# One transposing load for four token tiles, in a routed mixture of experts

## The chip, the cores and the metric

The kernel runs on one core of one Trainium2 chip. The metric is the device time of one execution in microseconds (us), as the median of several runs. [...]

## What is computed

The input `x` has 8 sequences of 3584 tokens with 192 channels, all float32. First a causal convolution of seven taps runs along each sequence; its taps are a softmax over one weight row per head, and each of the 8 heads owns 24 channels. The 28672 rows of the result then go through a mixture of 8 experts with one expert for each token:

```python
xn = x / (norm(x) + 1e-6); en = expert_emb / (norm(expert_emb) + 1e-6)
logits = xn @ en.T / tau
e = argmax(logits);  gate = softmax(logits)[e]
out = gate * (relu(x @ w1[e]) @ w2[e])       # w1: 192 x 1024, w2: 1024 x 192
```

## The kernel before, in words

Tokens are worked on in 16 chunks of 1792 (`CT`): 16 tiles (`NT`) of 112 tokens (`TP`), one token a partition. Chunk by chunk there are two parts.

The first part prepares and routes. `load_x` brings the chunk's rows (one DMA of about 1.5 MB, with a small one ahead where a sequence begins). `mix` runs the convolution as matmuls with a band matrix (L389), copies the result back over the input (L392) and sums squares (L402, L405). `scaled` multiplies four tiles (a group, `GX`) by a power of two and casts them to float16 into `rows2` (L436, L438); `rest` adds the float16 remainders that keep near-float32 precision and repeats 64 columns (L445, L448, L451). `rows2` holds two chunks; a token's row has 240 words of 32 bits there (`RW`): 448 float16 columns, then the token's number and its gate (words 224 and 225), then zeros. `turn` transposes a group: the first 384 float16 columns of each of its four tiles become three blocks of 128 channels by 112 tokens in `xtb`, a ring of four groups. `logits` multiplies these blocks by the expert embeddings (L612), `rank` finds each token's expert, its gate and its row in a list sorted by expert, and `put` sends the rows of one tile to that list in DRAM, `rows_d`, with an indirect DMA from GpSimd (L628). The first two chunks are transposed on TensorE instead (L499, L503), and their groups lie in the same ring.

The second part runs the experts over blocks of 128 to 512 rows of one expert. `fetch` reads the block's place (L745) and loads its rows from `rows_d`, transposed, with two DMAs on SyncE's queue (L753), and a small load of numbers and gates (L757). The loads name the scatters that they need. Three blocks are held. `expert` then runs the first product with five matmuls for each of eight column chunks (L799), the ReLU on ScalarE (L803) and its float16 remainder on VectorE (L805), then the second product for each 128 rows (L822), the gate on ScalarE (L827, into `y`, a ring of four tiles of 128 by 192 float32), and an indirect DMA from GpSimd to the output (L829). The first product's five PSUM banks (`h`) serve the second product too.

Which blocks are run is chosen while the chunks still come in: after chunks 2, 3, 5, 8 and 12 (`PICK`), and at the end, `hand_out` or `last_blocks` calls `pick` and that `select`, a chain of some twenty tiny VectorE instructions on one partition (L663 to L712). It writes `sel`, which SyncE (L745), TensorE and VectorE read for each block.

The order of the work is planned in Python: `run` walks through an expert's steps, counts a clock of its own, and draws steps of the routing in between. After the last `turn` of a chunk the plan waits 14 of its microseconds (`TURN`) before the logits. SyncE's instructions stay in the order in which they are written: turn of groups 0 and 1, `load_x` of the chunk two ahead, turn of groups 2 and 3, and the fetches between them. The other engines' instructions are put in order by the tile framework with a simulated timeline, and each engine runs its list in order.

GpSimd's DMAs build their descriptors in a scratch area of SBUF, 8192 bytes a partition.

Of the kernel before, what the change touches and what calls it, by code (L numbers as in the profile page):

```python
# [12 lines left out]
F16 = mybir.dt.float16  # L13
# [12 lines left out]
D = 192  # L26
# [5 lines left out]
CT = TP * NT  # L32
XD = 224
RW = 240


W2 = 3 * F
# [5 lines left out]
NFC = F // 128  # L43
PICK = (2, 3, 5, 8, 12)
GX = 4
XW = GX * 3 * TP
NACT = 3
PRE = 39
TURN, RANK, GAP = 14.0, 10.0, 0.5
# [26 lines left out]
class _Moe:  # L76
    def __init__(self, ctx, tc, x, weight, emb, tau, w1, w2, out):
        self.tc, self.nc = tc, tc.nc
        self.x, self.weight, self.emb, self.tau = x, weight, emb, tau
        self.w1, self.w2, self.out = w1, w2, out  # L80
        B, S, _ = x.shape
        self.B, self.S, self.N = B, S, B * S
        self.nch = self.N // CT
        self.per_b = S // CT
        self.cap = self.N + PAD
        self.dummy = E * self.cap
        pool = lambda name, bufs, **k: ctx.enter_context(
            tc.tile_pool(name=name, bufs=bufs, **k))
        self.cp = pool("const", 1)
        self.xp = pool("xload", 2)  # L90
        self.sp = pool("small", 2)
        self.lp = pool("lone", 1)
        self.ep = pool("expert", 3)
        self.yp = pool("y", 3)
        self.op = pool("out", 4)
        self.mp = pool("meta", 6)
        self.rings = {k: pool("ps_" + k, n, space=PSUM)
                      for k, n in (("r", 2), ("l", 1), ("h", 5))}

        self.res = self.cp.tile([128, E * RES], F16, name="res")  # L100
        self.work = self.cp.tile([128, 2 * NFC * 512 + S2 + RES - W2], F16, name="work")
        self.hid = self.work[:, 0:2 * NFC * 512]
        self.slot = self.work[:, 2 * NFC * 512:]
        self.xtb = self.cp.tile([128, NT // GX, XW + HALO], F16, name="xtb")
        self.rows2 = self.cp.tile([TP, 2, NT, RW], I32, name="rows2")
        self.ids = self.cp.tile([TP, NT], I32, name="ids")
        self.xtn = 0
        self.wexp = self.cp.tile([128, E, 2], I32, name="wexp")
        self.dp = pool("scratch", 1, space=DRAM)
        self.rows_d = self.dp.tile([E * self.cap + PAD, RW], I32, name="rows_d")  # L110
        self.scatters, self.pend, self.step = [], [], None
        self.nput, self.final = 0, False
        self.counts, self.pace = {}, 1.0
        self.xts, self.mixed = [], {}
        self.subs, self.ready, self.at, self.copied = [], 0, 0, 0
        self.clock, self.mm = 0.0, None
# [50 lines left out]

    def constants(self):
        nc, cp = self.nc, self.cp
        nc.gpsimd.memset(self.xtb[:, :, XW:], 0.0)  # L170
        nc.gpsimd.memset(self.rows2[:, :, :, XD + 2:], 0)
        nc.gpsimd.iota(self.ids, pattern=[[TP, NT]], base=TP - 1,
                       channel_multiplier=-1)
        head = self.ep.tile([128, 4 * 512], F16, tag="xT", name="head")[:].bitcast(F32)
        self.idf, self.onef = head[:, 0:128], head[:, 128:256]
        make_identity(nc, self.idf)
        self.idh = cp.tile([128, 128], F16, name="idh")
        nc.vector.tensor_copy(out=self.idh, in_=self.idf)
        nc.gpsimd.memset(self.onef, 1.0)
        self.oneh = cp.tile([128, 128], F16, name="oneh")  # L180
        nc.gpsimd.memset(self.oneh, 1.0)

        self.lth = cp.tile([128, 128], F16, name="lth")
        nc.gpsimd.memset(self.lth, 1.0)
        nc.gpsimd.affine_select(
            out=self.lth, in_=self.lth, pattern=[[1, 128]], base=0,
            channel_multiplier=-1, compare_op=ALU.is_gt, fill=0.0)

        tmp = self.op.tile([128, D], F32, tag="y", name="tmp")[:, 0:2 * E + 64].bitcast(I32)
        e8i = tmp[0:TP, 0:E]  # L190
        nc.gpsimd.iota(e8i, pattern=[[-1, E]], base=E, channel_multiplier=0)
        self.e8 = cp.tile([TP, E], F32, name="e8")
        nc.vector.tensor_copy(out=self.e8, in_=e8i)

        self.rst = cp.tile([TP, E, NT], F32, name="rst")
        nc.gpsimd.memset(self.rst, 1.0)
        nc.gpsimd.memset(self.rst[:, :, 0:1], 0.0)

        nums = tmp[0:1, E:E + 64]
        nc.gpsimd.iota(nums, pattern=[[1, 64]], base=0, channel_multiplier=0)  # L200
        self.nums = cp.tile([1, 64], F32, name="nums")
        nc.vector.tensor_copy(out=self.nums, in_=nums)

        cbi = tmp[:, E + 64:]
        nc.gpsimd.iota(cbi, pattern=[[self.cap, E]], base=0, channel_multiplier=0)
        self.cb = cp.tile([128, E], F32, name="cb")
        nc.vector.tensor_copy(out=self.cb, in_=cbi)

        self.start = cp.tile([1, E], F32, name="start")
        nc.vector.tensor_copy(out=self.start, in_=cbi[0:1, :])  # L210
# [231 lines left out]
    def rest(self, c, g):  # L442
        xc, u = self.mixed[c][0], slice(g * GX, g * GX + GX)
        rows = self.rows2[:, c % 2].bitcast(F16)
        self.nc.vector.tensor_tensor(  # L445
            out=rows[:, u, 0:128], in0=xc[:, u, 0:128],
            in1=rows[:, u, 128:256], op=ALU.subtract)
        self.nc.vector.tensor_tensor(  # L448
            out=rows[:, u, 320:384], in0=xc[:, u, 128:192],
            in1=rows[:, u, 256:320], op=ALU.subtract)  # L450
        self.nc.vector.tensor_copy(out=rows[:, u, 384:448], in_=rows[:, u, 256:320])  # L451


    def route(self, c):
# [23 lines left out]
    def first(self, c):  # L478
# [9 lines left out]
        for v in steps:  # L488
# [4 lines left out]
            else:  # L493
# [4 lines left out]
                for a in range(GX):  # L498
# [2 lines left out]
                        in_=rows[:, g * GX + a, k * 128:(k + 1) * 128],  # L501
                        identity=self.idh[:TP, :TP])
                nc.scalar.copy(  # L503
                    out=xT[:, 0:XW].rearrange("p (a k t) -> p a k t", k=3, t=TP)[:, :, k, :],
                    in_=tp)
                if k == 2:
                    if g == 0:
# [6 lines left out]
    def rank(self, c, lg, f):  # L514
# [63 lines left out]
        di = sp.tile([TP, NT], I32, tag="di", name="di")  # L578
        nc.vector.tensor_single_scalar(out=di, in_=dr, scalar=-1.0, op=ALU.add)
        yield 0.8, 0.0  # L580
        self.pend += [(c, di[:, t:t + 1], r32[:, t, :]) for t in range(NT)]
        self.left += CT
        if c + 1 in PICK[1:]:
            self.hand_out(c + 1)
# [23 lines left out]
    def logits(self, lg, xT, g):  # L608
        for a in range(GX):
            for k in range(3):  # L610
                u = (a * 3 + k) * TP
                i = self.nc.tensor.matmul(  # L612
                    out=lg[:, g * GX + a, :], lhsT=xT[:, u:u + 128],
                    rhs=self.mb if k == 2 else self.ma,
# [4 lines left out]

    def turn(self, c, g):  # L620
        xT, rows, t = self.xt_next(), self.rows2[:, c % 2].bitcast(F16), g * GX
        xv = xT[:, 0:XW].rearrange("p (a k t) -> p a k t", k=3, t=TP)
        for a in range(GX):
            self.nc.sync.dma_start_transpose(out=xv[:, a], in_=rows[:, t + a, 0:2 * D])
        return xT

    def scatter(self, idx, src):
# [29 lines left out]
    def select(self, n, k, last, name, cb):  # L657
# [17 lines left out]
        nc.vector.scalar_tensor_tensor(out=bs, in0=ap, scalar=-float(n),  # L675
                                       in1=self.start, op0=ALU.mult, op1=ALU.add)
        jf = self.nums[:, 0:k]
        ge, df = one("ge", (1, k, E + 1), F16), one("df", (1, k, E))
        nc.vector.memset(ge, 1.0)
        nc.vector.tensor_tensor(  # L680
            out=ge[:, :, 1:], in0=a[:].unsqueeze(1).to_broadcast([1, k, E]),
# [3 lines left out]
        nc.vector.tensor_tensor(  # L685
            out=df, in0=df, in1=bs[:].unsqueeze(1).to_broadcast([1, k, E]),
            op=ALU.mult)
        ro, tm, se = one("ro", (1, k)), one("tm", (1, k)), one("se", (1, k))
        nc.vector.tensor_reduce(out=ro, in_=df, op=ALU.add, axis=AX.X)
        nc.vector.scalar_tensor_tensor(out=ro, in0=jf, scalar=float(n), in1=ro,  # L690
                                       op0=ALU.mult, op1=ALU.add)
# [353 lines left out]
```

## Time and profile before

| | us |
|---|---|
| median of 3 runs (lowest, highest) | 1233.92 (1232.15, 1236.98) |
| the profiled execution | 1238.18 |
| its span, first to last instruction | 1236.5 |
| TensorE matmul busy | 1127.5 (91%) |
| VectorE busy | 756.1 (61%) |
| ScalarE busy | 587.4 (48%) |
| GpSimd busy | 550.4 (45%) |
| mean granted TensorE clock | 0.955 |

Busy time of TensorE is from the start of a matmul to its modelled end, so it is no measure of peak speed, but the time in which it has nothing under way is idle time. The transposing loads of `turn` lie between 124.7 and 766.7 us of the span. Before that the weights are prepared and the first two chunks are routed; after it, only experts' blocks are left.

### The profile page before, as it was taken

Reading aid. Unit: us, or ns where it says so; the run is one execution under the profiler, and the core shown is the slowest. Engines: PE = TensorE matmul, PEld = TensorE weight load, DVE = VectorE, ACT = ScalarE, POOL = GpSimd, SP = SyncE. Lnnn points to the kernel's source line nnn. Section 1 sums busy time; section 2 is a strip of 40 time slices with the busy share of each in tenths; the row PEclk is TensorE's granted clock in tenths of the full one; section 3 lists DMA queues with packets and bytes.
Section 4 is the critical chain, followed back from the end, with each engine's and each line's share of the span. In section 5 each row is a group of like instructions: output and inputs, shape, how many; then the busy total and the mean of one; then the engine's idle time right before and its main releaser. Section 6 shows DMA issues by size and latency. Waiting matters only on the chain.

```text
span 1236.5 us, 31375 instructions
## 1 busy us (share of the span) xinstructions
PE 1127.5 (91%) x10428; PEld 872.4 (71%) x10428; DVE 756.1 (61%) x2029; ACT 587.4 (48%) x1350; POOL 550.4 (45%) x522
## 2 busy tenths in 40 slices
PE   4675769899999899998989999999999999999998
PEld 2553658786677876756877676666677777898897
DVE  2899766886668757666675746553434453466365
ACT  4986445554554555563635454423333333333333
POOL 0074165574575645565745546673222222222222
PEclk9676879899999999999989999999999999999999
DMA  9945566576675576755638545326122231123121
GB/s 243 231 131 157 119 157 150 126 164 122 150 173 146 109 158 134 161 144 107 164 73 191 110 86 134 90 87 107 43 54 49 52 72 49 44 48 71 43 57 43
DMA packets 305818, 140.68 MB, mean 114 GB/s; under 512 B 247630, under 2 KB 296141, under 8 KB 305664
## 3 DMA queue, kind: packets, MB, share of 16 engines
q1 hardware_dynamic: 282000, 87.97, 34.3%
q0 software_dynamic: 23664, 50.68, 14.5%
q8 instruction: 94, 1.54, 0.5%
q14 instruction: 60, 0.49, 0.1%
HBM read 38.35 MB, written 51.05 MB: 72 GB/s over the span
## 4 chain that ended last, share of the span: by engine, by line
PE 37%; issue 8%; POOL 3%; DMA 3%; ACT 1%; DVE 1%; POOLq 0%; ACTq 0%; DVEq 0%
PE h_ps L799 18%; PE o_ps L822 17%; POOL out_dram L829 2%; POOL rows_d L628 1%; PE conv_ps L389 1%; DMA rows_d<-rows,di 1%; DMA xtb<-rows 1%; DMA out_dram<-y,e_mt 1%; ACT work L803 1%; DVE work L805 0%; DMA rows_d<-xtb,padi 0%; ACT rows L438 0%; ACT sq L402 0%; PE lg_ps L612 0%; DVE work L735 0%
## 5 line engine op out<-in xcount | busy, mean ns | idle before, releaser
L822 PE MATMUL o_ps<-work 128*128 128x192 f16 x5472 | 497.8, 248 | 21.3 <-DVE work L805 9.9
L822 PEld LDWEIGHTS <-work 128*128 128x128 f16 x5472 | 458.5, 99 | 59.9 <-DVE work L805 15.9
L829 POOL DMA_INDIRECT out_dram<-y,e_mt x228 | 255.1, 1119 | 470.8 <-ACT y L827 434.0
L805 DVE SCALAR_TENSOR_TENSOR work<-h_ps,work 128x512 f16<-128x512 f32 x456 | 311.1, 687 | 169.0 <-ACT work L803 165.2
L803 ACT ACTIVATE work<-h_ps 128x512 f16<-128x512 f32 x456 | 267.5, 596 | 236.5 <-PE h_ps L799 205.5
L628 POOL DMA_INDIRECT rows_d<-rows,di x256 | 281.6, 1100 | 141.4 <-issue 56.8
L799 PE MATMUL h_ps<-e_xT,res 128*128 128x512 f16 x1360 | 312.3, 382 | 6.9 <-DVE work L805 3.5
L799 PEld LDWEIGHTS <-res 128*128 x1360 | 131.8, 98 | 162.0 <-issue 19.7
L799 PE MATMUL h_ps<-e_xT,work 128*128 128x256 f16 (+1 forms) x2200 | 226.7, 259 | 15.2 <-DMA e_xT<-rows_d 10.2
L799 PEld LDWEIGHTS <-work 128*128 128x128 f16 x2200 | 187.4, 99 | 41.5 <-DMA e_xT<-rows_d 10.4
L827 ACT ACTIVATE y<-o_ps,g 128x192 f32<-128x192 f32 x228 | 92.8, 418 | 236.2 <-PE o_ps L822 209.7
L735 DVE COPY work<-res 128x3074 f16 x85 | 82.3, 968 | 165.2 <-PE o_ps L822 161.2
L389 PE MATMUL conv_ps<-xt,band 128*112 128x384 f32 x256 | 110.8, 534 | 14.9 <-ACT xt L392 8.0
L438 ACT CAST rows<-xt 112x768 f16<-112x768 f32 x64 | 53.0, 832 | 97.3 <-DMA rows_d<-rows,di 44.5
L392 ACT COPY xt<-conv_ps 112x384 f32<-112x384 f32 x128 | 60.3, 479 | 43.7 <-PE conv_ps L389 41.2
L402 ACT ACTIVATE sq<-xt 112x192 bf16<-112x192 f32 x204 | 73.6, 361 | 4.8
L445 DVE TENSOR_TENSOR rows<-xt,rows 112x512 f16<-112x512 f32 x64 | 44.2, 690 | 45.0 <-ACT rows L438 42.5
L389 PEld LDWEIGHTS conv_ps<-xt,band 128*112 128x112 f32 x256 | 42.7, 193 | 33.3 <-issue 14.5
L436 DVE TENSOR_TENSOR xt<-xt,x_p_s 112x768 f32<-112x768 f32 x64 | 58.6, 953 | 0.0
L732 DVE COPY work<-res 128x3072 f16 x56 | 53.7, 960 | 0.2 <-PE h_ps L799 0.2
L612 PEld LDWEIGHTS <-xtb 128*128 128x128 f16 x768 | 30.2, 98 | 26.7 <-DMA xtb<-rows 13.2
L612 PE MATMUL lg_ps<-ma,xtb 128*128 128x16 f16 x512 | 31.0, 171 | 14.3 <-ACT xtb L503 7.5
(158 smaller groups left out, 524.7 us busy)
## 6 DMA issues: line engine op xcount, KB each, us to landing
xt<-in_dram SPq DMA_DIRECT2D x8, 1536.0 KB
xt<-in_dram SPq DMA_DIRECT2D x7, 1440.0 KB
rows_d<-rows,di POOLq DMA_INDIRECT x256
out_dram<-y,e_mt POOLq DMA_INDIRECT x228
xtb<-rows SPq DMA_TRANSPOSE x224
res<-in_dram SPq DMA_DIRECT2D x4, 768.0 KB
work<-in_dram SPq DMA_DIRECT2D x4, 768.0 KB
e_xT<-rows_d SPq DMA_TRANSPOSE x184
```

Source lines behind the costliest of these rows:

```text
L389: self.behind(nc.tensor.matmul(out=ps, lhsT=self.band[:, h, :], rhs=xt[:, :, h * G:(h + 1) * G], start=True, stop=True))
L392: nc.scalar.copy(out=xc[:, :, h * G:(h + 1) * G], in_=ps)
L402: nc.scalar.activation(out=sq, in_=xc[:, t, :], func=AF.Square, accum_out=n2[:, t:t + 1])
L612: i = self.nc.tensor.matmul(out=lg[:, g * GX + a, :], lhsT=xT[:, u:u + 128], rhs=self.mb if k == 2 else self.ma, start=(k == 0), stop=(k = ...
L628: i = self.nc.gpsimd.indirect_dma_start(out=self.rows_d[:, :], out_offset=bass.IndirectOffsetOnAxis(ap=idx, axis=0), in_=src, in_offset=No ...
L735: self.nc.vector.tensor_copy(out=self.slot[:, S2:], in_=self.res[:, bass.ds(self.we + W2, RES - W2)])
L799: mm = nc.tensor.matmul(out=ps[:, c, :], lhsT=w1(o, b + c), rhs=xT[:, k, :], start=(i == 0), stop=(i == 4))
L803: self.step = nc.scalar.activation(out=hh[:, b:b + m, :], in_=ps, func=AF.Relu).ins
L805: nc.vector.scalar_tensor_tensor(out=hl[:, b:b + m, :], in0=ps, scalar=0.0, in1=hh[:, b:b + m, :], op0=ALU.max, op1=ALU.subtract)
L822: mm = nc.tensor.matmul(out=o, lhsT=h[:, c, q], rhs=w2[:, c, k:k + D], start=(c + i == 0), stop=(c == NFC - 1 and i == 2))
L827: self.step = nc.scalar.activation(out=y, in_=o, func=AF.Copy, scale=g[:, a:a + 1]).ins
L829: i = nc.gpsimd.indirect_dma_start(out=self.out[:, :], out_offset=bass.IndirectOffsetOnAxis(ap=mt[:, a, 0:1], axis=0), in_=y, in_offset=No ...
```

## The change

The rows in `rows2` get 256 words, so that a group's four tiles are, in each partition, one run of 2048 float16 columns: 16 blocks of 128. `turn` loads a group with one transposing DMA in place of four. A tile has four blocks in `xtb` now, of which the fourth (the repeated columns, the word pair and zeros) is not used by the logits; the 16 columns behind a tile's third block, which the third block's matmul reads along, lie at the start of the fourth. The scatters still send 240 words of a row. L451 copies 68 columns a tile in place of 64, so that the word pair is written before the transpose reads it.

Room for this is made in two places: the scratch for GpSimd's descriptors is 4096 bytes a partition, and the larger temporary tiles of `select` (`ge`, `df`, and `ro`, `tm`, `se` inside the first) are taken from the ring of `y`.

```diff
+SW = 256
-XW = GX * 3 * TP
+XW = GX * 4 * TP
...
-        self.xtb = self.cp.tile([128, NT // GX, XW + HALO], F16, name="xtb")
-        self.rows2 = self.cp.tile([TP, 2, NT, RW], I32, name="rows2")
+        self.xtb = self.cp.tile([128, NT // GX, XW], F16, name="xtb")
+        self.rows2 = self.cp.tile([TP, 2, NT, SW], I32, name="rows2")
...
-        nc.gpsimd.memset(self.xtb[:, :, XW:], 0.0)
+        nc.gpsimd.memset(self.xtb[:].rearrange(
+            "p h (a k t) -> p (h a) k t", k=4, t=TP)[:, :, 3, 0:HALO], 0.0)
...
-        self.nc.vector.tensor_copy(out=rows[:, u, 384:448], in_=rows[:, u, 256:320])
+        self.nc.vector.tensor_copy(out=rows[:, u, 384:452], in_=rows[:, u, 256:324])
...
-        self.pend += [(c, di[:, t:t + 1], r32[:, t, :]) for t in range(NT)]
+        self.pend += [(c, di[:, t:t + 1], r32[:, t, 0:RW]) for t in range(NT)]
...
-                u = (a * 3 + k) * TP
+                u = (a * 4 + k) * TP
...
     def turn(self, c, g):
         xT, rows, t = self.xt_next(), self.rows2[:, c % 2].bitcast(F16), g * GX
-        xv = xT[:, 0:XW].rearrange("p (a k t) -> p a k t", k=3, t=TP)
-        for a in range(GX):
-            self.nc.sync.dma_start_transpose(out=xv[:, a], in_=rows[:, t + a, 0:2 * D])
+        self.nc.sync.dma_start_transpose(
+            out=xT.rearrange("p (n t) -> p n t", t=TP),
+            in_=rows[:, t:t + GX, :].rearrange("p a c -> p (a c)"))
         return xT
...
-        ge, df = one("ge", (1, k, E + 1), F16), one("df", (1, k, E))
+        tmp = self.op.tile([128, D], F32, tag="y", name="sl_ge")[0:1]
+        ro, tm, se = (tmp[:, i * k:(i + 1) * k] for i in (5, 6, 7))
+        ge = tmp.bitcast(F16)[:, 0:k * (E + 1)].rearrange("p (k e) -> p k e", e=E + 1)
+        df = self.op.tile([128, D], F32, tag="y", name="sl_df")[0:1, 0:k * E].rearrange(
+            "p (k e) -> p k e", e=E)
...
-        ro, tm, se = one("ro", (1, k)), one("tm", (1, k)), one("se", (1, k))
...
-                    dynamic_dma_scratch_size=8192)
+                    dynamic_dma_scratch_size=4096)
```

## Rows read from the trace of the kernel before

**Rows 1.** The page's part 2: tenths in 40 slices of 30.9 us.
```profile
PE   4675769899999899998989999999999999999998
PEclk9676879899999999999989999999999999999999
DMA  9945566576675576755638545326122231123121
```

**Rows 2.** Waits of PE: us in total, times, longest.
```profile
PE lg_ps L612 <- DMA xtb<-rows: 11.7, 9, 3.7
...
PE h_ps L799 <- DMA e_xT<-rows_d: 10.2, 2, 6.0
```

**Rows 3.** Source lines L624 and L753: SyncE's time for one, ns min/median/max.
```profile
L624 SPq DMA_TRANSPOSE xtb<-rows x224: 1174/1252/4145, 124.7 to 766.7; - x112
...
L753 SPq DMA_TRANSPOSE e_xT<-rows_d x184: 1130/1236/2622, 113.0 to 1229.9; - x184
```

**Rows 4.** Timeline, chunk 2's first turn: start, us, instruction, idle before.
```profile
124.73 10.27 SPq L624 DMA_TRANSPOSE xtb<-rows  x8
...
127.09 0.21 PE L612 MATMUL lg_ps<-ma,xtb 128*128 128x16 f16 x2 [3.67 <-DMA xtb<-rows]
```

**Rows 5.** Windows, one quiet fetch: busy of the engines, PEclk, DMA share, GB/s.
```profile
1053.50:1054.00 0.50, 0.50 (x9) 0.50 (x7) 0.00 (x0) 0.00 (x0) 0.00 (x0) 1.00 0.79 172
```

**Rows 6.** Timeline, chunk 3's second turn and the fetch behind it.
```profile
164.77 0.52 SPq L373 DMA_DIRECT2D xt<-in_dram  x1
165.39 12.24 SPq L624 DMA_TRANSPOSE xtb<-rows  x8
...
173.67 0.22 PE L612 MATMUL lg_ps<-ma,xtb 128*128 128x16 f16 x2 [3.08 <-DMA xtb<-rows]
...
178.41 2.53 SPq L753 DMA_TRANSPOSE e_xT<-rows_d  x2
...
181.51 4.87 PE L799 MATMUL h_ps<-e_xT,work 128*128 128x256 f16 x22 [6.02 <-DMA e_xT<-rows_d]
```

**Rows 7.** Windows there: last three columns PEclk, DMA share, GB/s.
```profile
168.00:170.00 2.00, 2.00 (x33) 2.00 (x30) 1.94 (x19) 0.81 (x5) 1.39 (x3) 1.00 1.07 349
170.00:172.00 2.00, 0.59 (x14) 0.36 (x10) 2.00 (x4) 0.42 (x1) 2.00 (x1) 1.00 1.22 348
...
180.00:185.00 5.00, 3.49 (x17) 2.50 (x18) 2.56 (x11) 0.83 (x1) 3.78 (x5) 0.50 0.95 146
```

**Rows 8.** Timeline, chunk 4's second turn and the fetch behind it.
```profile
209.24 14.72 SPq L624 DMA_TRANSPOSE xtb<-rows  x8
...
224.83 2.53 SPq L753 DMA_TRANSPOSE e_xT<-rows_d  x2
...
228.94 2.32 PE L799 MATMUL h_ps<-e_xT,work 128*128 128x256 f16 x10 [4.16 <-DMA e_xT<-rows_d]
```

**Rows 9.** Window right behind it, columns as in Rows 5.
```profile
230.00:235.00 5.00, 5.00 (x38) 3.76 (x37) 3.10 (x8) 1.19 (x2) 3.20 (x4) 0.56 0.70 161
```

**Rows 10.** Timeline, chunk 6's second turn.
```profile
308.28 12.89 SPq L624 DMA_TRANSPOSE xtb<-rows  x8
...
321.89 0.18 PE L612 MATMUL lg_ps<-mb,xtb 128*128 128x16 f16 x1 [1.53 <-DMA xtb<-rows]
```

**Rows 11.** Waits of SyncE's queue: us in total, times, longest.
```profile
SPq L364 <- DVE rows L448: 25.1, 3, 10.4
```

**Rows 12.** Groups by line and form: VectorE's copy in `rest`.
```profile
L451 DVE COPY rows<-rows 112x256 f16<-112x256 f16 x64 | 14.1, 221 | 0.0
```

**Rows 13.** Timeline, `select` after chunk 2 and at the end, and `y`.
```profile
186.97 0.16 DVE L704 CAST sel<-sl_se 1x7 int32<-1x7 f32 x1 [2.11 <-SPq L745]
...
814.84 0.15 DVE L705 CAST sel<-sl_ro 1x8 int32<-1x8 f32 x1
...
827.42 0.42 ACT L827 ACTIVATE y<-o_ps,g 128x192 f32<-128x192 f32 x1 [5.38 <-DMA out_dram<-y,e_mt]
```

**Rows 14.** Timeline, GpSimd in a run of scatters.
```profile
181.75 0.94 POOL L628 DMA_INDIRECT rows_d<-rows,di  x1 [0.30 <-ACT rows L438]
```

More of the change, by code (lines that the diff above doesn't have):

```diff
@@ L503, in first @@
                 nc.scalar.copy(
-                    out=xT[:, 0:XW].rearrange("p (a k t) -> p a k t", k=3, t=TP)[:, :, k, :],
+                    out=xT[:, 0:XW].rearrange("p (a k t) -> p a k t", k=4, t=TP)[:, :, k, :],
                     in_=tp)
```

## The prediction

> **What bounds the kernel now.** I read the page's row of slices first: TensorE is 0.8 busy or more from the seventh slice on, nearly always at full clock, while it has holes in the first six, where the clock falls as well [rows 1]. So TensorE sets the end, and a change on SyncE's queue can only be worth what TensorE waits for that queue. The second view is TensorE's waits: it stood 11.7 us for the transposing loads of `turn` and 10.2 us for the experts' loads [rows 2]. This is the ceiling, 22 us, with some more where the clock falls behind a hole. The third view, the source lines, says why the loads come late: SyncE is held 1.25 us by each, and as long by a load of an expert's block: over blocks of 128 to 512 rows the median is 1.24 and the least 1.13 [rows 3]. Sixteen loads a chunk hold it 20 us or more, and whatever stands behind them waits. Then I went through the timeline of the four places that hold nearly all of this waiting.
>
> **The change, part by part.** A group's four loads become one. For 14 chunks that is 56 loads in place of 224. The issue time did not move with the size in the trace, so I take 1.25 us for one, which frees SyncE of 168 x 1.25 = 210 us; by itself this is worth nothing, since SyncE isn't the bound. The load moves 112 x 2048 x 2 = 459 KB where the four moved 344 KB. The nearest row for the speed is a fetch of a 512-row block with nothing beside it, 172 GB/s in its busiest half microsecond [rows 5]: 2.7 us, estimated. From issue to the first matmul the old load took 127.09 - 124.73 = 2.36 us [rows 4], of which 1.25 is issue, 0.5 its own 86 KB at that speed, and 0.6 the rest. The new one: 1.25 + 2.7 + 0.6 = 4.5 us.
>
> Place A, chunk 2's first turn [rows 4]. TensorE waits from 123.4. The first tile came at 127.09, the fourth after 3 x 1.28 more, at 130.9; the matmuls of the second product lay between them. Now all four come at 124.73 + 4.5 = 129.3: the first wait is 2.2 us longer, and the short ones for the second and third tile, at most the spacing of the issues (10.27/8 = 1.28) each, are gone. I take 0, with -2 and +3 as ends.
>
> Place B, chunk 3's second turn [rows 6]. Eight loads stand behind `load_x`'s 1.5 MB, and the fetch of the next block behind all of them. TensorE idles 3.08 us for the logits and then 6.02 us for the block. The DMA engines moved 348 GB/s there [rows 7]; 1.5 + 2 x 0.46 = 2.4 MB take 6.9 us, so the two loads land near 172.5 and SyncE is free at about 173, against 177.6. The fetch issues there in place of 178.41 and TensorE begins 3.1 us later as before, at 176.1 against 181.51. I take -5; the ends are 0 (something else holds the fetch) and -9 (both waits gone). The granted clock is 0.50 while TensorE works on after the hole [rows 7]; a hole of 5 us will leave it there, so nothing is taken for the clock.
>
> Place C, chunk 4's second turn [rows 8]. The loads hold SyncE from 209.24 to 223.96 and the fetch follows at 224.83; TensorE waits 4.16 us. By the sum for B the loads are through by 218, and the block is there by 221, before TensorE wants it at 228.94 - 4.16 = 224.8: -4.2. The hole is gone, and with it the clock of 0.56 in the five busy microseconds behind it [rows 9], 5 x 0.44 = 2.2 us. Together -6.4, ends 0 and -6.4.
>
> Place D, chunk 6 [rows 10]: eight loads of 12.89 us end after the planned 14 us, and a logit waits 1.53 us. Two loads behind `load_x` take some 8 us: -1.5, ends 0 and -3.5 (with the clock).
>
> What is late next: SyncE comes sooner to `load_x`, which waits until VectorE has read the older chunk (25.1 us in three waits now [rows 11]); that wait grows, but it ends when it ended, so the fetches behind are not later than before.
>
> The 33% more bytes: the DMA engines are 0.5 to 0.7 busy in those slices [rows 1]; scatters and fetches share them. I take 0, with +3 as the upper end (a seventh of the 22 us of waits, as rough as that).
>
> L451 copies 272 columns for 256: 221 ns x 16/256 = 14 ns, 64 times, 0.9 us on VectorE [rows 12], beside TensorE's work; if the odd width cost it as much again as it takes now, 14 us over 700, still beside it. At nothing. The two memsets run once, at the start.
>
> The scratch. In a run of scatters GpSimd starts one every 1.24 us, 0.94 busy and 0.30 between [rows 14], and no wait for space shows. Half the scratch could only cost where that spacing grows; from below it is 0. From above: each of the last chunk's 16 scatters and 9 pads a microsecond later, some +25 us before the last blocks may load, hidden as far as blocks are still held. I take 0, the nearest row.
>
> `select`'s tiles. This is the one added wait: a tile in the ring of `y` waits until the output scatter of the `y` four places back has landed, and the next `y` in that place waits until `select` is done with it. That VectorE instruction has the remainders (L805) queued behind it, the `y` on ScalarE the ReLUs; both hold PSUM banks that TensorE needs. Two places matter. After chunk 2 the last writes of `sel` run only at 186.97, behind SyncE's read [rows 13], with one `y` place held until then. At the end four selects follow each other, the third done at 814.84 [rows 13], while an expert's four `y` are due; after that the `y` wait for their scatters anyway until 827.42 [rows 13], which hides most. I take +3 in all, ends 0 and +28 (below, the third rival).
>
> The sum: 0 - 5 - 6.4 - 1.5 + 3 = -10 us. The profiled execution took 1238.2 (span 1236.5), so 1228.2. It stands 4.3 above the median of the runs, 1233.9; the same step from the median gives **1224 us**.
>
> [...] In the trace a transposing load holds SyncE 1.24 us in the median over sources of 128 to 512 rows and one or three column blocks [rows 3]. [...]
>
> **Rivals.** *All of it stays.* Both waits of B go, the clock behind B comes back, and `select` costs nothing: -9 - 6.4 - 3.5 - 2 = -21, 1213 us. For it: TensorE has no other long wait in those stretches. Against: B's `load_x` bytes go first whatever SyncE does.
>
> *The transfers are hidden behind another wait.* Fetches stand behind `load_x`, whose wait for VectorE ends no sooner [rows 11], and the engines' order comes out of a simulation that a changed load shifts. Then only D and the clock of C are left, with `select` against it: -1.5 - 2.2 + 2 = -2, 1232 us.
>
> *`select` in the ring of `y` costs more than the loads give (slower).* Place: the end, around 815 us, and the hand-outs after chunks 2, 5, 8 and 12. An expert's four `y` wait for the third and fourth select, their products hold four of five banks, and TensorE stands up to 10 us; after chunk 2 one bank short until 187, up to 6; at the other three a first select of some 4 us (twenty instructions of 0.16 us [rows 13] and their gaps), 12. Together +28, less 13: +15, 1249 us. It decides from 13 us on. Against: the framework's order can put a late `y` behind other work, and five banks cover a few microseconds.
>
> *The load isn't one load in time (slower).* If its issue goes by column blocks, 1.25/3 x 16 = 6.7 us, two hold SyncE 13.4 us where eight held it 10.3 to 14.7 [rows 4, 6, 8, 10]. A loses 3, B and C 2 each, D 1: +8, 1242 us. Against it: the flat issue time [rows 3].
>
> **How the numbers follow.** The forecast 0.48 (own range 1216 to 1230), all stays 0.15, hidden 0.20, `select` 0.11, not one load 0.06. A change under 0.5% (6.2 us) can't be told from none. Faster, below 1227.7: 0.42 of the forecast's 0.48, 0.15, and 0.03 of the hidden case: 0.60. Slower, above 1240.1: 0.10 of `select` and 0.05 of the last: 0.15. Same: 0.25. The range of eight in ten goes from 1208, past the case in which all stays, to 1241, which leaves out most of the two slower cases.
>
> **What would show it.** `turn`'s line with 56 loads of 1.2 to 2.5 us each; TensorE's wait for the experts' loads at 10.2 us going to 4 or less, and for `turn` to 6 or so, nearly all of it at place A; the fetch behind chunk 4's second turn issued before 219 and the clock full from there; the last load of `turn`, issued at 766.7 now [rows 3], some 13 us earlier. `y` waiting on `select`, or VectorE on an output scatter in front of `select`'s first fill, would show the third rival; a `turn` row near 6 us the fourth. The forecast is wrong if the fetches at B and C move and TensorE's holes stay, or if holes of the same size open elsewhere before 785.

## The result, and the profile after

The changed kernel takes 1249.95 us (median of six runs, 1248.88 to 1251.8); the kernel before, run beside it, 1234.81 (six runs, 1232.15 to 1239.95). The ratio is 1.0111, with a 95% interval of 1.009 to 1.0132: the change costs 1.1%, where a gain of 10 us was forecast. The profiled execution has a span of 1247.9 us, against 1236.5 before.

The page's slices first, as in [rows 1], 31.2 us each here.

```profile
PE   4666879789998899998989899979999999999998
PEclk9666979898998899999999999998999999999999
DMA  9845957857878494864848647324222231123122
```

TensorE's holes in the first six slices are filled in part only (67576 behind the first 4 before, 66687 now); the 27th slice, 811 to 842 us, fell from 9 to 7. The second view, TensorE's waits (us in total, times, longest), answers to [rows 2].

```profile
PE h_ps L804 <- ACT y L832: 14.5, 6, 3.6
PE o_ps L827 <- ACT work L808: 13.7, 7, 3.4
...
PE h_ps L804 <- DVE work L810: 10.2, 5, 8.4
PE h_ps L804 <- DMA e_xT<-rows_d: 7.8, 1, 7.8
...
PE o_ps L827 <- DVE work L810: 4.3, 12, 1.2
...
PE lg_ps L614 <- DMA xtb<-rows: 1.4, 1, 1.4
```

The same waits on other engines in the kernel before:

```profile
PE o_ps L822 <- DVE work L805: 9.9, 17, 2.4
...
PE o_ps L822 <- ACT work L803: 6.5, 6, 1.8
...
PE h_ps L799 <- ACT y L827: 5.1, 2, 4.3
...
PE h_ps L799 <- DVE work L805: 3.5, 4, 1.1
```

So the edit to the loads did what it says. TensorE waited 11.7 us in nine waits for the transposing loads of `turn`, and waits 1.4 in one. But 7.8 of the 10.2 us for the experts' loads are left, and three waits on other engines have grown: the first product's on `y` to 14.5 us (5.1 before) and on the remainders to 10.2 (3.5), the second product's on the ReLUs to 13.7 (6.5). These 23.3 us more are of the kind that the forecast named as what would make it wrong, holes of the same size elsewhere, though two of them, 8.4 and 1.8 us, lie behind the 785 us that it named. One wait has shrunk, the second product's on the remainders, from 9.9 to 4.3 us. In all, TensorE's idle time rose from 109.0 us (1236.5 - 1127.5) to 118.3 (1247.9 - 1129.6), which is 9.3 of the 11.4 us that the span grew by. A single line of such a list moves by some 3 us from one execution to another: E4, whose instructions stand in the order of the kernel before, has 6.6 us where that has 3.5.

The line of the load, beside [rows 3] (ns min/median/max), and places A and C, beside [rows 4] and [rows 8]:

```profile
L624 SPq DMA_TRANSPOSE xtb<-rows x56: 1422/2816/10266, 124.0 to 762.6; - x56
```

```profile
128.24 0.21 PE L614 MATMUL lg_ps<-ma,xtb 128*128 128x16 f16 x2 [1.36 <-DMA xtb<-rows]
...
201.70 5.72 SPq L624 DMA_TRANSPOSE xtb<-rows  x2
...
208.84 13.26 SPq L624 DMA_TRANSPOSE xtb<-rows  x2
...
223.08 2.54 SPq L758 DMA_TRANSPOSE e_xT<-rows_d  x2
...
227.52 0.59 PE L804 MATMUL h_ps<-e_xT,work 128*128 128x256 f16 x2 [7.75 <-DMA e_xT<-rows_d]
```

Read the durations against what stands ahead. A chunk's first two loads follow a fetch and hold SyncE 5.72 us here; the second two follow the 1.5 MB of `load_x` and hold it 13.26, hardly less than the eight small ones did (14.72). Over the twelve chunks with a `load_x` between the pairs, the first pair takes 3.8 to 5.7 us (once 14.4, of which 10.6 lie between the two loads) where eight took 10.3 to 11.5 (once 15.1); the second takes 9.1 to 13.3 where eight took 11.7 to 14.7. At place C the fetch goes out at 223.08, not at the 219 of the forecast, and the wait is longer than before.

The end, where the largest loss in one place lies: the first of the four last selects (VectorE), the first output scatter of the expert ahead of it in GpSimd's queue, and TensorE.

```profile
830.89 0.99 POOL L834 DMA_INDIRECT out_dram<-y,e_mt  x1 [0.30 <-issue]
...
833.32 0.08 DVE L685 MEMSET sl_ge<- 1x27 f16 x1 [5.92 <-DMA out_dram<-y,e_mt]
...
835.87 0.17 DVE L689 TENSOR_TENSOR sl_df<-sl_ge 1x24 f32<-1x24 f16 x1 [1.05 <-DMA out_dram<-y,e_mt]
...
843.46 2.29 PE L804 MATMUL h_ps<-e_xT,res 128*128 128x512 f16 x5 [8.43 <-DVE work L810]
...
847.53 8.13 PE L804 MATMUL h_ps<-e_xT,res 128*128 128x512 f16 x30 [1.78 <-ACT y L832]
```

A tile of `select` takes the place of one of the last expert's four `y`, all made by 818. That place is free when the `y`'s output scatter has landed, and the scatter is issued at 830.89 only, since GpSimd first works through nine pads and ten of the last chunk's row scatters at 1.25 us each. VectorE stands 5.92 us in front of a fill of 0.08 us, with the remainders queued behind it, and TensorE stands 8.43 us for a remainder. Its granted clock is 0.53 of full speed from 840 to 851 us; behind the hole of 6.02 us in [rows 6] it was 0.50 [rows 7].

To see where the rest went, I compared the start of the n-th of the 228 `y` on ScalarE in two traces, each counted from the start of its span. For the changed kernel against the kernel before, in us: -7.1 at the first (138 us), -3.6 at the 13th (213), +9.3 at the 45th (391), +6.3 at the 129th (809), +11.9 from the 137th (850) to the end. Some 6 us are lost by 809, in spite of all that the loads gave, and 5.6 at the last selects.

### The profile page after: what moved, and what is told of

It is laid out like the page before. It is cut to its first block, busy times and chain, and to the rows that moved or that the text cites. A ratio compares the mean times of both kernels' runs of the same rounds, so it can differ in the third digit from the quotient of the medians.

```text
span 1247.9 us, 31071 instructions
## 1 busy us (share of the span) xinstructions
PE 1129.6 (91%) x10428; PEld 876.1 (70%) x10428; DVE 758.3 (61%) x2029; ACT 587.2 (47%) x1350; POOL 548.3 (44%) x522
## 5 line engine op out<-in xcount | busy, mean ns | idle before, releaser
L827 PE MATMUL o_ps<-work 128*128 128x192 f16 x5472 | 501.6, 250 | 26.8 <-ACT work L808 13.7
L834 POOL DMA_INDIRECT out_dram<-y,e_mt x228 | 252.0, 1105 | 451.1 <-ACT y L832 410.0
L804 PE MATMUL h_ps<-e_xT,res 128*128 128x512 f16 x1360 | 311.4, 381 | 12.5 <-DVE work L810 10.2
L404 ACT ACTIVATION_READ_ACCUMULATOR sq<-xt 112x1 f32 x204 | 38.3, 188 | 0.0
```

Of the source, the lines that this page charges most:

```text
L404: nc.scalar.activation(out=sq, in_=xc[:, t, :], func=AF.Square, accum_out=n2[:, t:t + 1])
L804: mm = nc.tensor.matmul(out=ps[:, c, :], lhsT=w1(o, b + c), rhs=xT[:, k, :], start=(i == 0), stop=(i == 4))
L827: mm = nc.tensor.matmul(out=o, lhsT=h[:, c, q], rhs=w2[:, c, k:k + D], start=(c + i == 0), stop=(c == NFC - 1 and i == 2))
L834: i = nc.gpsimd.indirect_dma_start(out=self.out[:, :], out_offset=bass.IndirectOffsetOnAxis(ap=mt[:, a, 0:1], axis=0), in_=y, in_offset=No ...
```

## The experiments

Theories. *Ring*: `select`'s tiles in the ring of `y` cost the loss. *Load*: the one load costs it, by its hold of SyncE, its bytes or the changed schedule. *Scratch*: the halved scratch of the software DMAs does. Ratios are to the kernel before in the same job.

**E1, own tiles.** `select`'s tiles are taken from a pool of their own again. To make room for them the scratch goes to 2048.

```
-        tmp = self.op.tile([128, D], F32, tag="y", name="sl_ge")[0:1]
...
+        ge, df = one("ge", (1, k, E + 1), F16), one("df", (1, k, E))
...
+        ro, tm, se = one("ro", (1, k)), one("tm", (1, k)), one("se", (1, k))
...
-                    dynamic_dma_scratch_size=4096)
+                    dynamic_dma_scratch_size=2048)
```

> The changed kernel, except that select's tiles stand in a pool of their own again, as before the change; to make room for them the software DMAs' scratch is cut to 2048 (the fourth kernel tests that by itself). Ring theory (the tiles in the ring of y cost the loss: about 6 us at the last four selects, another 6 or so at the hand-outs): 1234 to 1240 us, near the kernel before or under it; VectorE's 5.92 us wait for an output scatter at the last selects is gone. Load theory (one large load, which holds SyncE and moves a third more bytes, costs it): 1246 to 1251. If both share it, about 1243.

Measured: 1232.94 us, 0.9954 (0.9936 to 0.9972). Not only is the loss gone; the kernel is 0.46% faster than before.

**E2, the ring alone.** The kernel before with `select`'s tiles from the ring, as the change has them, and no other edit.

```
-        ge, df = one("ge", (1, k, E + 1), F16), one("df", (1, k, E))
+        tmp = self.op.tile([128, D], F32, tag="y", name="sl_ge")[0:1]
...
+        df = self.op.tile([128, D], F32, tag="y", name="sl_df")[0:1, 0:k * E].rearrange(
+            "p (k e) -> p k e", e=E)
```

> The kernel before with one edit: select's tiles come from the ring of y, as in the change; four loads a group and the scratch of 8192 stay. Ring theory: 1243 to 1250 us, with a wait of VectorE for an output scatter ahead of a select's first fill near the end. Load theory and scratch theory: 1234 to 1236, as the kernel before.

Measured: 1251.97 us, 1.0111 (1.0095 to 1.0127), the ratio of the whole change. Near the end its trace repeats the two rows of the changed kernel, at other times:

```profile
834.98 0.08 DVE L683 MEMSET sl_ge<- 1x27 f16 x1 [5.89 <-DMA out_dram<-y,e_mt]
...
845.10 2.29 PE L802 MATMUL h_ps<-e_xT,res 128*128 128x512 f16 x5 [8.36 <-DVE work L808]
```

One kernel with the ring and nothing else, and one with everything but the ring: together they show the ring as the cause.

**E3, four wide loads.** The changed kernel with one load for each token tile, out of the same 256-word rows.

```
+        for a in range(GX):
+            self.nc.sync.dma_start_transpose(
+                out=xT[:, a * 4 * TP:(a + 1) * 4 * TP].rearrange(
+                    "p (n t) -> p n t", t=TP),
+                in_=rows[:, t + a:t + a + 1, :].rearrange("p a c -> p (a c)"))
```

> The changed kernel with four loads of one token tile each in place of one load of four, from the same 256-word rows into the same layout: as many bytes, select's tiles in the ring, scratch of 4096. Load theory, by the time that one load holds SyncE behind the row loads: 1236 to 1242. Load theory, by the bytes (a third more of them): 1247 to 1251, as the changed kernel. Ring theory: 1244 to 1251, about as the kernel with only the ring.

Measured: 1255.7 us, 1.0139 (1.0121 to 1.0157). That is above every range expected. The changed kernel has 1.0111 (1.009 to 1.0132) in its own job. The two intervals overlap a little, so that the one load is a gain even here is likely by this pair, and not shown.

**E4, the scratch alone**, in the kernel before.

```
-                    dynamic_dma_scratch_size=8192)
+                    dynamic_dma_scratch_size=2048)
```

> The kernel before with the software DMAs' scratch cut to 2048, a quarter, and nothing else; the instructions of every engine stand in the same order. Scratch theory (half the scratch costs a share of the loss, as GpSimd waits for space in its runs of scatters): 1237 us or more, with the scatters 1.3 us apart or more in place of 1.24. Ring and load theory: 1234 to 1236.

Measured: 1237.34 us, 1.0000 (0.9987 to 1.0012). The scratch costs nothing, and E1 is read without it.

**E5 and E6, the ring at the end alone and at the hand-outs alone.** The kernel before with a condition, in E5 that of the diff, in E6 its opposite.

```
+        if self.final:
+            tmp = self.op.tile([128, D], F32, tag="y", name="sl_ge")[0:1]
...
+        else:
+            ge, df = one("ge", (1, k, E + 1), F16), one("df", (1, k, E))
```

> The kernel before with select's tiles from the ring of y in the four selects at the end alone; the hand-outs' selects keep their own tiles. Times against the kernel before in the same job. Ring theory, its two places independent: 6 to 7 us slower (0.5 to 0.6%), as the kernel with the whole ring lost 6.6 us between the 128th and the 136th y; all of it lost between 805 and 860. Rival (the loss at the end is only what the late hand-outs carry there, or a shift in the engines' order): within 2 us of before.

> The kernel before with select's tiles from the ring of y in the hand-outs alone (after chunks 2, 5, 8 and 12); the four selects at the end keep their own. Ring theory, its two places independent: 7 to 9 us slower (0.6 to 0.7%), lost by the hand-outs after chunks 2 and 8 mainly, and nothing more from 805 on. Rival (the end alone costs): within 2 us of before.

Measured: E5 1242.29 us, 1.0042 (1.0018 to 1.0065); E6 1244.46, 1.0055 (1.0034 to 1.0076). Both places cost, and 0.42 + 0.55% is near the 1.11% of E2. E5 has the end's rows, E6 has none of them:

```profile
823.08 0.08 DVE L687 MEMSET sl_ge<- 1x27 f16 x1 [5.93 <-DMA out_dram<-y,e_mt]
...
833.12 2.29 PE L806 MATMUL h_ps<-e_xT,res 128*128 128x512 f16 x5 [8.32 <-DVE work L812]
```

The start of the n-th `y` against the kernel before, in us, says the same place by place (E17 and E18 are told below):

```
n     before  changed   E1     E2     E5     E6     E7    E17     E4    E18
0      137.8    -7.1   -7.7   -1.1   -3.3   -0.1   -6.6   -6.8   -1.6   -7.9
4      160.3    +3.1   -3.8   +8.2   -1.8   +8.0   -0.3   +3.3   -0.9   -4.5
12     213.5    -3.6   -8.3    0.0   -1.1    0.0   +0.1   -3.5   -0.6   -9.2
16     241.9    +1.0   -4.2   +2.7   -2.0   +3.2   +4.7   -3.2   -1.4   -6.6
24     287.5    +3.3   -4.8   +5.2   -2.9   +7.5   +4.1   -0.3   -1.6   -8.3
40     372.9    -0.6   -8.5   +5.5   -3.0   +7.3   +0.1   -4.2   -1.3  -11.4
44     390.8    +9.3   -4.6  +11.5   -3.0  +13.3   +4.2   +5.8   -1.2   -9.4
48     414.5    +2.4   -5.8   +4.8   -2.9   +6.8   +3.2   -1.1   -1.8  -10.6
64     501.2    +4.3   -5.8   +8.3   -0.5  +10.4   +2.9   +2.1   +0.9  -10.1
128    809.2    +6.3   -1.8   +8.0   -3.9   +9.1   +6.4   +6.3   -1.3   -9.0
136    849.8   +11.9   -1.7  +14.6   +2.2   +9.1   +6.7   +5.1   -1.2  -10.9
224   1220.9   +11.9   -1.7  +14.6   +2.2   +9.1   +6.7   +5.4   -1.2  -10.8
```

From 128 to 136, the last selects: +6.6 in E2, +6.1 in E5, +5.6 in the changed kernel, 0.0 in E6 and +0.1 in E1. E4 has the order of the kernel before, so its column, between -1.8 and +2.6 us over all 228 `y`, tells how far two executions differ. At 4, the first hand-out, E2 and E6 jump by 9.3 and 8.1, E5 by 1.5 and E1 by 3.9; at 44 E2 and E6 jump by 6.0, E5 not at all, and E1 gives back 3.9. But a late `y` is not yet lost time: both jumps are gone again at 12 (0.0 in E2 and in E6) and at 48. What these two kernels keep comes between 12 and 24, 5.2 us in E2 and 7.5 in E6. There E6's TensorE waits 6.9 us for the block at place C (4.2 before), and from 245 to 300 us 4.9 us for a ReLU (0.7 before); its selects of the second hand-out fill their tiles at 246.6 and 257.6. The 3.6 us more between 48 and 64 are hardly the ring's, since E4 and E5 have 2.7 and 2.5 of them. With one load the first hand-out keeps its loss: the changed kernel is 4.7 us behind E1 at 12, and 8.1 at 128. (Row 0 lies before any of the ring's tiles in E5, whose -3.3 there is none of its edit.)

**E7 and E8, the load of rows behind all four transposing loads**, in E1's kernel (one load) and in the kernel before (four).

```
-        if c + 2 < self.nch:
-            self.load_x(c + 2)
         for g in range(2, NT // GX):
             xTs.append(self.turn(c, g))
+        if c + 2 < self.nch:
+            self.load_x(c + 2)
```

> The first kernel of the study (one load a group, select's tiles of their own, scratch of 2048) with one line moved: the load of the rows of the chunk after next is issued behind all four transposing loads of a chunk, not between the second and the third. Theory A (a transposing load holds SyncE until its data can go, so what stands ahead in the queue is its price): the second pair of loads takes 4 to 6 us in place of 9 to 14, the fetch behind chunk 4's loads comes some 6 us sooner, TensorE's wait of 3.9 us for the expert's load goes, and the time is 1227 to 1231 where before is 1236. Theory B (the loads' issue time is bound by something else, or TensorE's time is given back at the ReLUs and remainders): the second pair stays above 8 us, or it falls and the time stays at 1232 to 1235.

> The kernel before with the same line moved and nothing else: four loads a group, the load of rows behind all sixteen. Theory A: the last eight loads take 10.3 to 11.5 us in place of 11.7 to 15, since four small loads are bound by their own issue of 1.25 us and only the excess goes: 0 to 4 us faster than before. Theory B: no faster; 1235 to 1238.

Measured: E7 1241.63 us, 1.0038 (1.0024 to 1.0052); E8 1241.68, 1.0031 (1.0014 to 1.0047). Theory A holds for the hold and fails for the time. With no load of rows ahead, four big loads in a row hold SyncE some 10 us, and a pair 5 (E7's timeline of SyncE; some later groups take 10.3 to 21.6 us, with SyncE waiting between their loads). No single load takes more than 3.9 us there, against 6.4 to 10.3 for each that follows `load_x` in the changed kernel, so the price of the second pair was the queue ahead of it:

```profile
124.49 10.04 SPq L624 DMA_TRANSPOSE xtb<-rows  x4
...
200.64 9.74 SPq L624 DMA_TRANSPOSE xtb<-rows  x4
...
305.66 5.19 SPq L624 DMA_TRANSPOSE xtb<-rows  x2
```

The wait for an expert's block at place C is gone from E7's waits, and the kernel is 0.8% slower than E1 by the two ratios all the same: the rows come later, and the waits among the engines grew (for the ReLUs to 16.5 us, 13.9 in E1). In E8 the wait for experts' blocks grew as well, to 16.6 us in four waits (10.2 in two before). So the two runs price the move as a whole, and not the shorter hold by itself. Of E7's waits:

```profile
PE o_ps L824 <- ACT work L805: 16.5, 10, 3.7
...
PE h_ps L801 <- DVE work L807: 8.7, 6, 4.7
PE conv_ps L391 <- ACT xt L394: 7.7, 4, 4.8
...
PE conv_ps L391 <- DMA xt<-in_dram: 4.1, 1, 4.1
...
PE o_ps L824 <- DVE x_r_t L149: 3.3, 1, 3.3
```

**E9 to E12 and E13 to E16, places and loads.** Both jobs ran on chips where the kernel before took 1329.13 and 1320.34 us, and where TensorE also stood 30 to 44 us for "issue" on the line of the second product; of these runs only ratios within a job are read. E10's and E13's wait lists show it (before has 1.3 us of such waits in all):

```profile
PE o_ps L822 <- issue: 30.6, 32, 2.5
```

```profile
PE o_ps L827 <- issue: 43.9, 59, 2.9
```

E9 is the changed kernel with six places for `y` and the scratch at 2048; E10 the kernel before with the same; E11 E1's kernel with five places; E12 E1's kernel with four wide loads, by the diff of E3.

```
-        self.op = pool("out", 4)
+        self.op = pool("out", 6)
```

> The changed kernel with six places in the ring of y in place of four, and the scratch at 2048 to make room; select's tiles stay in the ring. Ring theory as a wait (a tile of select takes the place of the y four back, whose output scatter stands in GpSimd's queue among pads and row scatters; with six places it is that of the expert before, landed long ago): VectorE's wait of 5.9 us ahead of a select's fill near the end goes to under 1 us, and the time is 1233 to 1241 where before is 1237. Rival (the tiles in the ring cost by the order that they give to VectorE's instructions, not by a wait for a place): 1246 to 1251.

> The kernel before with six places in the ring of y and the scratch at 2048; select's tiles of their own, four loads a group. The control for the kernel with six places: if the y themselves wait for a place, 1232 to 1235; if not, 1236 to 1239, as before, and what six places give the changed kernel is all select's.

> The first kernel of the study (one load a group, select's own tiles, scratch of 2048) with five places in the ring of y. If the waits of h_ps on y (6.3 us in four waits there) are waits for a place: 1229 to 1232 where before is 1237. If they are waits for ScalarE itself, or are given back: 1232 to 1235, as that kernel.

> The first kernel of the study with four loads of one token tile each in place of one: 256-word rows and a third more bytes, select's own tiles, scratch of 2048. The price of the wide rows by itself against before. By the pair with the ring (four wide loads 1.0139 of before, four narrow ones 1.0111): 1239 to 1242, 0.2 to 0.4% slower, so that the one load gives back some 8 us. If that pair differed only in the engines' order: 1235 to 1238.

Measured: E9 1.0082 (1.0054 to 1.011), E10 0.9993 (0.9969 to 1.0016), E11 0.9938 (0.991 to 0.9965), E12 1.008 (1.0053 to 1.0108). E10 says that `y` by itself has no use for more places. E9 lies where its expectation puts the rival, the order of the engines, and not the wait for a place.

E13, E14 and E16 are E9, E12 and E11 again; E15 is E1's kernel with two loads of two token tiles each.

```
+        for a in range(0, GX, 2):
+            self.nc.sync.dma_start_transpose(
+                out=xT[:, a * 4 * TP:(a + 2) * 4 * TP].rearrange(
+                    "p (n t) -> p n t", t=TP),
+                in_=rows[:, t + a:t + a + 2, :].rearrange("p a c -> p (a c)"))
```

> The changed kernel with six places in the ring of y in place of four and the scratch at 2048; select's tiles stay in the ring. If the loss is a wait for a place, at the end and at the hand-outs: 0.995 to 1.001 of before, as the kernel with own tiles, and no wait of VectorE for an output scatter ahead of a select's fill. If the end is a wait for a place and the hand-outs cost by the order of the engines: 1.003 to 1.007, with nothing lost between 805 and 860. If all of it is order: 1.009 to 1.013.

> The kernel with one load a group and select's own tiles (0.9954 of before), with four loads of one token tile each in place of one: 256-word rows and a third more bytes. If the wide rows cost: 1.002 to 1.005 of before, by the pair with the ring (1.0139 against 1.0111). If they don't: 0.999 to 1.001, and then the one load's gain is all that there is to gain.

> The same kernel with two loads of two token tiles each in place of one of four. If SyncE's hold goes by loads (1.25 us each) while nothing stands ahead of them: a first pair of groups takes 5 to 6 us, about as with one load a group (3.8 to 5.7), and the time is 0.994 to 0.998 of before. If it goes by bytes: 4 us and as fast as one load. If the time is set by what TensorE waits for among the other engines and not by the loads: 0.995 to 1.002, with the loads early and no less idle on TensorE.

> The kernel with one load a group and select's own tiles, with five places in the ring of y. If the waits of h_ps on y (6.3 us in four) are waits for a place: 0.990 to 0.993 of before. If they are waits for ScalarE, or are given back: 0.994 to 0.998, as with four places.

Measured: E13 1.0031 (1.0 to 1.0061), E14 1.0069 (1.0039 to 1.0099), E15 0.9945 (0.9916 to 0.9975), E16 0.9934 (0.9902 to 0.9966). Four wide loads are slower than four narrow ones in both jobs: on these chips the wide rows cost 0.7 to 0.8%, more than by E3 against E2 (0.28%, with intervals that overlap). The larger loads give back more than that, and E15's two loads can't be told from E16's one (E16 has five places for `y`, E15 four). E13, the same kernel as E9, lies lower, where its expectation puts a wait at the end and an order at the hand-outs; E17 is the third try. Of SyncE's hold, E15 and E14 show how it goes with the size (ns min/median/max):

```profile
L625 SPq DMA_TRANSPOSE xtb<-rows x112: 1222/1351/5952, 133.1 to 795.8; - x112
```

```profile
L625 SPq DMA_TRANSPOSE xtb<-rows x224: 1184/1262/3598, 133.5 to 823.9; - x112
```

One token tile 1.26 us in the median, two 1.35, four 2.8 in the changed kernel and 2.2 in E7, where no load of rows goes between: nearly flat at first, then not.

**E17 and E18, six places with the ring and five without, in one job.**

> The changed kernel with six places in the ring of y and the scratch at 2048, once more. All of the loss a wait for a place: 0.995 to 0.999 of before. The end a wait for a place, the hand-outs something else: 1.001 to 1.006, with nothing lost at the end. All of it order: 1.009 to 1.013.

> One load a group, select's own tiles, five places in the ring of y, scratch of 2048, once more: 0.990 to 0.996 of before, by the two earlier ratios of 0.9938 and 0.9934. If those were peculiar to chips that hold TensorE for issue: 0.995 to 0.998, as with four places.

Measured: E17 1243.41 us, 1.0046 (1.0028 to 1.0065); E18 1230.92, 0.996 (0.9938 to 0.9982), with before at 1237.77. E18 fits both of its expected ranges: five places can't be told from E1's four (0.9954). Six places mend the end and not the hand-outs: in the table E17 has +6.3 at 128, as the changed kernel has, and no loss behind it. At the end one of E17's fills still waits, that of the last select and not of the first; it falls beside an expert's second product on TensorE (from 826.63, 8.09 us), and TensorE's waits there stay at 1.5 us or less:

```profile
826.63 8.09 PE L827 MATMUL o_ps<-work 128*128 128x192 f16 x96 [0.32 <-DVE sl_t L713]
...
833.37 0.22 DVE L685 MEMSET sl_ge<- 1x189 f16 x1 [5.30 <-DMA out_dram<-y,e_mt]
...
842.78 1.36 PE L804 MATMUL h_ps<-e_xT,res 128*128 128x512 f16 x5 [1.52 <-DVE work L810]
```

At the first hand-out the changed kernel and E17 look alike. Of the changed kernel:

```profile
159.92 1.25 PE L804 MATMUL h_ps<-e_xT,work 128*128 128x256 f16 x10 [2.00 <-DVE sl_av L665]
...
162.79 1.07 ACT L832 ACTIVATE y<-o_ps,g 128x192 f32<-128x192 f32 x3
...
163.25 4.43 PE L804 MATMUL h_ps<-e_xT,work 128*128 128x256 f16 x20 [2.08 <-ACT y L832]
```

Of E17, with six places:

```profile
160.12 1.25 PE L804 MATMUL h_ps<-e_xT,work 128*128 128x256 f16 x10 [2.00 <-DVE sl_av L665]
...
162.99 1.34 ACT L832 ACTIVATE y<-o_ps,g 128x192 f32<-128x192 f32 x4
...
163.45 4.42 PE L804 MATMUL h_ps<-e_xT,work 128*128 128x256 f16 x20 [2.08 <-ACT y L832]
```

Of E1, the same part of the work:

```profile
156.56 0.42 ACT L829 ACTIVATE y<-o_ps,g 128x192 f32<-128x192 f32 x1 [0.92 <-PE o_ps L824]
...
158.15 4.53 PE L801 MATMUL h_ps<-e_xT,work 128*128 128x256 f16 x40
...
158.58 0.41 ACT L829 ACTIVATE y<-o_ps,g 128x192 f32<-128x192 f32 x1
```

In E1 ScalarE makes each `y` as its product ends (156.56, 158.58), between the Squares of the next chunk, and TensorE runs the next expert's product in one piece. With the ring, three or four `y` stand behind the row of Squares, at 162.8 to 163.0, after the first steps of `select` on VectorE. Their PSUM banks stay taken, and TensorE stops twice for 2 us. No engine waits for an output scatter between 150 and 168 us. So at this hand-out it is an order of instructions in which the late `y` stand behind other work, and six places leave it as it is. No run gave these `y` their old place in the order with `select`'s tiles still in the ring, so the order is read from the traces, and what it costs is argued.

## Why the prediction was wrong

**The step that failed** is the term of `select`'s tiles: "I take +3 in all, ends 0 and +28". Alone it measures +14.6 us in E2's profile and 1.11% of the time (0.95 to 1.27%, some 14 us). It was judged from two rows, and the judgement was that later waits of `y` hide most of it. The third rival named the cause, the two places and 1249 us. Its working was less good than its number: it priced the end at 10 us and the hand-outs at 18 (the runs: 6 and 8 to 9) and set 13 against them for the loads.

Two things in its mechanism were the other way round. At the end it isn't first of all `y` that waits for `select`: `select` waits for a `y`'s scatter, behind GpSimd's queue, with VectorE's remainders behind it. The prediction did give this as a sign of the third rival, but didn't price it. Its rows were there: the 25 scatters that the prediction counts, at 1.24 us each [rows 14], and a `y` held 5.38 us for an output scatter at 827.42 [rows 13]. And at the hand-outs the objection raised against the rival, that the framework's order can put a late `y` behind other work, is what the first hand-out shows, and it doesn't help there. The later hand-outs were not read so closely.

**The loads** were forecast at 0 - 5 - 6.4 - 1.5 = -13 us; E1 gives 0.46% (0.28 to 0.64%) of 1237, some 6. Place by place, by E1's column: A and B together -8.3 by the 13th `y`, more than the -5 of the sum and near its other end of -9. B's wait is gone, as forecast: in the changed kernel the pair is through at 158.6, and TensorE's one wait for a block is that of place C. But from `load_x`'s issue at 148.27 this took 10.4 us, not the 8.2 of the forecast (164.77 to 173). C is +4.1 where -6.4 stood (+2.6 in E18). The step "the loads are through by 218" took the second pair to be quick once its bytes can flow, and in the changed kernel it holds SyncE to 222.1, in E1 (203.86 + 11.55) to 215.4. E1 keeps a wait of 3.92 us for that block. The sign was there: [rows 3] has 4.1 us as the longest of 224 equal loads, and of the twelve above 2.8 us eleven stand right behind a `load_x`. E7 shows that the queue ahead makes the hold (no load above 3.9 us there), and that taking it away by loading the rows later gains nothing (1.0038). D and what follows reach -8.5 by the 41st `y`, and most of it is given back, down to -1.8 by the 129th. This is one execution, of 1236.31 us where E1's median is 1232.94; E18's, of 1227.39 with a median of 1230.92, still has -9.0 at the 129th, so how much is given back is known only roughly. E1's list:

```profile
PE o_ps L824 <- ACT work L805: 13.9, 7, 3.2
...
PE h_ps L801 <- DVE work L807: 5.8, 6, 2.9
...
PE h_ps L801 <- DMA e_xT<-rows_d: 3.9, 1, 3.9
...
PE lg_ps L614 <- DMA xtb<-rows: 2.4, 2, 1.3
```

The first of these waits, the second product's on the ReLUs, is the one that has clearly grown: 13.9 us in E1 and 13.0 in E18, against 6.5 before and 5.8 in E4. That on the remainders (3.5 before, 6.6 in E4, 2.4 in E18) can't be told from none. This is the limit that the prediction put at nothing: TensorE got its data sooner, and stood longer for ScalarE, which had been nearly in time.

**The load's own time.** Forecast 4.5 us from issue to the first matmul at place A, measured 128.24 - 124.0 = 4.2. The flat issue time failed: 2.8 us in the median, not 1.25, and 2.2 in E7. These 1 to 1.6 us more contain waits behind other transfers: E7's 56 loads, all of one size, run from 1.42 to 3.88 us. The least holds, 1.42 against 1.17 us, differ by 0.25 only, which speaks for the queue ahead, and not the size, as most of the excess. TensorE came to A 3.5 us later than before (126.9 against 123.4) and so stood 1.4 us there, not 5.8.

**Right as forecast:** the scratch at nothing (E4, 1.0000, at an even smaller size). The wide rows were put at 0 to +3 us: E3 against E2 gives 3.7 in the profile, and E12 and E14 more than twice that, so the value of 0 was too low.

## What to carry to other kernels

A scratch tile taken from another loop's ring inherits that ring's release, here a DMA issued by a busy queue, and hands it to whatever is queued behind the tile's first write (here VectorE stood 5.92 us and TensorE 8.43); look up when the last owner's reader ends before calling the place free. It also changes the order that a scheduler gives to the ring's owner, and more places didn't mend that here (E17: still +6.3 us at the 129th `y`). Fewer and larger loads gave little more than a third of the waits that they removed (E1: 15.6 us of waits, 5.7 of time), and the wait for ScalarE's ReLUs grew by 7.4. Of the versions run, those with larger loads and `select`'s own tiles beat the kernel before: one load a group (E1 0.9954, with five places for `y` 0.996, 0.9938 and 0.9934) and two (E15 0.9945), which can't be told apart.

## What was not expected of the hardware

The time that a transposing load of 459 KB holds its queue isn't its own: 1.4 us at the least, 2.2 in the median with nothing big ahead (E7), 6.4 to 10.3 us for one right behind 1.5 MB of rows. Four such loads with nothing ahead hold it 10 us, as long as the eight small ones of [rows 4]. And on two of the five chips of the experiments the same program took 7% more time. There TensorE waited 30 to 44 us for "issue" on one line; in E10 it is 55.9 us over four lines, and the matmuls are busy 28 us longer than in the kernel before. Why is open. Open too is which part of the later hand-outs' loss is order and which is waiting: only the first was read closely, and of its loss nothing lasts in E2 and E6.
